# Two attention layers on one core: queries of two batches from one matmul of 288 columns

## The chip, the core and the metric

The kernel runs on one core of a Trainium2 chip. The core has a matmul engine (PE, with its weight loads listed as PEld), VectorE (DVE), ScalarE (ACT), GpSimd (POOL), and DMA queues; here SyncE (SP) issues nearly all transfers. The engines run side by side, each through its own list of instructions in order, and wait for one another by semaphores. The metric is the time of one execution in microseconds (us) on the device.

## The reference, cut to what matters

Two attention layers A and B of the same shapes, each with its own x, caches and weights, and their outputs beside each other:

```
x [16, 144, 448], wq [448, 16*256], k_cache and v_cache [16, 16, 512, 256], wo [16*256, 448]   (bf16)
q = (x @ wq) as [batch, head, 144, 256]
p = softmax(q @ k_cache^T / 16);  o = p @ v_cache
out[..., 0:448] of layer A, out[..., 448:896] of layer B = (heads of o side by side) @ wo
```

## The kernel before, in words

**Units and slots.** A unit U is one batch and one head of one layer: 512 units, 256 for each layer, in the order that `unit` (from L231) gives: batch by batch with its 16 heads, but for the first 32, where batches 0 and 1 are mixed. The program is written out by a loop over slots i, from -8 to 511 and a little beyond. In slot i unit i is finished, and the steps of later units are put beside it: this sets the order of each engine's list. One slot in the middle holds on PE, in this order:

- Q (`t_q`, L411): the query of unit i+15, transposed, x @ wq for 256 columns of Wq in two chunks of 128: eight matmuls of 144 columns (four pieces of the 448 rows of Wq by two chunks), into the PSUM bank qp_ps. `t_evac_q` (L425 on DVE, L429 on ACT) scales it by 1/16 into `qt_sb`, slot U % 12; DVE does it in slots i with i % 8 in 2, 4, 6, 7, ACT in the others.
- SB (`t_sb`, L459), in every eighth slot (i % 8 = 3): the scores of the last 32 query rows of eight units, four packed into one pass of the array.
- SA (`t_sa`, L536): the scores of the first 112 query rows of unit i+5, two matmuls of 512 columns, into one of the two banks sa_ps. Then DVE takes the maximum (`t_max`, L548) and ACT the exponential with its row sum (`t_exp`, L559).
- TA (`t_ta`, L590): four transposes of the probabilities of unit i+2 into sa_ps, which DVE copies to `pt_sb` (L600). Between exponential and TA lie the reciprocal (DVE, L569) and the division by the sum (POOL, L577). TB (`t_tb`, L513) does the same for the 32-row part, in two of eight slots.
- PV (`t_pv`, L623): the probabilities by V for unit i, eight matmuls of 144 columns; ACT copies the result into `ring` (L638, L640).
- OP (`t_op_piece`, L661): the output projection, matmuls of 448 columns for row chunks of 128 whose batches are finished. A credit of 2.25 matmuls per slot lets them out in twos (more from slot 482 on). The first chunk is ready in slot 25; where all ready chunks are done, a slot has no OP.

The 32-row part has its own maximum (L473), exponential (`t_exp_b`, L483, in the slots with i % 8 = 4 and 6, at the start of ACT's list for that slot) and reciprocal (L493).

**The plan of query slots.** `q_slot` gives the slot of each Q: eight in slot -7, one each in -5 to 2, two each in 4 to 7, then unit u in slot u-15. For units below 24 odd ones use the bank op_ps and even ones qp_ps (`q_bank`, L395), later ones qp_ps alone. A PSUM bank is guarded as a whole: a Q waits until the Q before it in the same bank is evacuated. In slots from 4 on the Qs stand at the start of the slot, one behind the other.

**Loads.** All loads are put in SP's list in the order of a deadline in slots (`plan`). K comes by DMA transposes for eight units at a time (L379), into one of three buffers, and occupies SP while it is issued; V (L392) for four units at a time, into one of three buffers, so a V load waits until PV of the units three groups earlier is done. x comes transposed for four batches at a time (L299, L300), into one of three buffers; the first four batches are loaded as they are and transposed on PE (`t_xt`, L336, copied out at L343): 12 transposes at the start, eight in slot 10. Wq lies once in the on-chip memory, in four parts of four heads (`t_load_wq`, L277 and L279); layer B's part goes in when the last Q of layer A that uses it is done, with deadlines 241, 245, 249 and 253, where its first Q stands. Wo (L287) likewise, in eight parts.

Of the kernel before, what the change touches and what calls it, by code (L numbers as in the profile page):

```python
# [5 lines left out]
BF16 = mybir.dt.bfloat16  # L6
# [116 lines left out]
def bass_concat_heads__mha_block_cached__gqa_block_cached__near_ridge_kernel(  # L123
# [54 lines left out]
    with contextlib.ExitStack() as es:  # L178
# [32 lines left out]
        x_nat = wo_flat[:, 8 * 4 * DH:8 * 4 * DH + 5 * D].rearrange("p (t e) -> p t e", t=5)  # L211
# [80 lines left out]

        def t_load_x(XG):
            pr, j = divmod(XG, Bn // XB)
            sl = XG % NXG
            x = xs[pr][j * XB:(j + 1) * XB].rearrange("b q d -> (b q) d")

            def e(q):
                q.dma_start_transpose(xt_sb[:, sl, 0:3, :], x[:, 0:384]).then_inc(sems["xt%d" % sl], 16)  # L299
                return q.dma_start_transpose(xt_sb[:, sl, 3, :], x[:, 320:448]).then_inc(sems["xt%d" % sl], 16)  # L300
            S.add(SP, e, writes=[(("xt", sl), XG)] + ([(("xt2", 0), 1)] if XG == NXG else []), dma_sem="xt%d" % sl, n_dma=2, name="x%d" % XG)

        def t_load_x_nat(k):
            x = xs[0][0:XB].rearrange("b q d -> (b q) d")
            sem = sems["xn%d" % k]

            def e(q):
                if k == 0:
                    return q.dma_start(x_nat[:, 0:3, :], x[0:384, :].rearrange("(t p) d -> p t d", p=128)).then_inc(
                        sem, 16)  # L310
                q.dma_start(x_nat[:, 3, :], x[384:512, :]).then_inc(sem, 16)
                return q.dma_start(x_nat[0:XB * SQ - 512, 4, :], x[512:XB * SQ, :]).then_inc(sem, 16)
            S.add(SP, e, writes=[(("xn", k), 0)], dma_sem="xn%d" % k, n_dma=1 + k, name="xn%d" % k)
# [10 lines left out]
        def t_xt(k):  # L324
            key, bank, acc = ((("sbb", 0), "sb0", ptb_ps[0]), (("sbb", 1), "sb1", ptb_ps[1]),
                              ("opp", "op", op_ps.bitcast(BF16)))[k]
            c0, n = ((0, 256), (256, 128), (384, XB * SQ - 384))[k]
            dst = acc[:, 0:4 * n].rearrange("p (c r) -> p c r", c=4)

            def e(t):  # L330
                ins = None
                for r0 in range(0, n, 128):
                    m = min(128, n - r0)
                    for kc in range(4):
                        d0 = min(128 * kc, D - 128)
                        ins = t.transpose(dst[:, kc, r0:r0 + m], x_nat[0:m, (c0 + r0) // 128, d0:d0 + 128],  # L336
                                          ident[0:m, 0:m])
                return ins
            S.add(PE, e, reads=[(("xn", k // 2), 0), ("ident", 0)], writes=[(key, ("x", k))], banks=[bank], name="XT%d" % k)

            def ev(v):
                o = xt_sb[:, 0, :, c0:c0 + n]
                return v.activation(o, dst, AF.Copy) if k == 1 else v.tensor_copy(o, dst)  # L343
            S.add(ACT if k == 1 else DVE, ev, reads=[(key, ("x", k))], writes=[(("xt2" if k == 2 else "xt", 0), 0)], banks=[bank],
                  name="ext%d" % k)
# [52 lines left out]
        def t_q(U):
            pr, b, h = unit(U)
            XG = (pr * Bn + b) // XB  # L400
            xsl = XG % NXG
            xo = (b % XB) * SQ
            hg = h // 4
            acc, key, bank = q_bank(U)

            def e(t):
                ins = None
                for kc in range(4):
                    for dc in range(2):
                        c0 = h * DH + dc * 128  # L410
                        ins = t.matmul(acc[:, dc * SQ:(dc + 1) * SQ], lhsT=wq_sb[:, kc, c0:c0 + 128],  # L411
                                       rhs=xt_sb[:, xsl, kc, xo:xo + SQ], start=(kc == 0 and dc == 0),
                                       stop=(kc == 3), skip_group_check=True)
                return ins
            S.add(PE, e, reads=[(("wq", hg), pr), ("wqz", 0), (("xt", xsl), XG)]
                  + ([(("xt2", 0), 0)] if XG == 0 and b > 1 else []),
                  writes=[(key, ("q", U))], banks=[bank], name="Q%d" % U)

        def t_evac_q(U):
            sl = U % NQT  # L420
            acc, key, bank = q_bank(U)
            src = acc[:, 0:2 * SQ].rearrange("p (c q) -> p c q", c=2)
            if (U - LQ) % 8 in (2, 4, 6, 7):
                def e(v):
                    return v.tensor_scalar(qt_sb[:, sl, :, :], src, 1.0 / 16.0, None, op0=ALU.mult)  # L425
                S.add(DVE, e, reads=[(key, ("q", U))], writes=[(("qt", sl), U)], banks=[bank], name="eq%d" % U)
            else:
                def e(a):
                    return a.activation(qt_sb[:, sl, :, :], src, AF.Copy, scale=1.0 / 16.0)  # L429
                S.add(ACT, e, reads=[(key, ("q", U))], writes=[(("qt", sl), U)], banks=[bank], name="eq%d" % U)  # L430
# [19 lines left out]
        def t_sb(SG):  # L450
            ksl = SG % NK

            def e(t):
                ins = None
                for dc in range(2):
                    for jj in range(8):
                        U = 8 * SG + jj
                        j = jj % 4
                        ins = t.matmul(sb_ps[jj // 4][32 * j:32 * j + 32, :].rearrange("q (k r) -> q k r", k=KR),  # L459
                                       lhsT=qt_sb[:, U % NQT, dc, QA:SQ],  # L460
                                       rhs=kt_of(U, dc), start=(dc == 0), stop=(dc == 1),
                                       tile_position=(0, 32 * j))
# [65 lines left out]
        def t_sa(U):  # L528
            SG = U // 8
            ksl = SG % NK  # L530
            bank = U % 2

            def e(t):
                ins = None
                for dc in range(2):
                    ins = t.matmul(sa_ps[bank][0:QA, :].rearrange("q (k r) -> q k r", k=KR),  # L536
                                   lhsT=qt_sb[:, U % NQT, dc, 0:QA],
                                   rhs=kt_of(U, dc), start=(dc == 0), stop=(dc == 1))
                return ins
            S.add(PE, e, reads=[(("qt", U % NQT), U)] + kt_keys([U]), writes=[(("sap", bank), ("s", U))],  # L540
# [166 lines left out]
        q_slot = [u - LQ for u in range(NT)]  # L707
        q_slot[0:24] = [-7] * 8 + [-5, -4, -3, -2, -1, 0, 1, 2] + [4, 4, 5, 5, 6, 6, 7, 7]
# [15 lines left out]
        for u in range(NT):  # L724
            at(q_at, q_slot[u], u)
# [3 lines left out]
        for XG in range(NXGT):  # L729
            pr, j = divmod(XG, Bn // XB)  # L730
            u_first = pr * NU + j * XB * H
            dl = u_first - LQ
            if XG >= NXG:
                pr0, j0 = divmod(XG - NXG, Bn // XB)
                lo = pr0 * NU + (j0 + 1) * XB * H - 1 - LQ + 1
            else:
                lo = s_min
            if XG:
                plan(lo, dl, 40, t_load_x, XG)
# [61 lines left out]
        while True:  # L801
# [10 lines left out]
            if i == q_slot[0]:  # L812
# [5 lines left out]
            for u in qs if not -LS <= i < 4 else ():  # L818
                t_q(u)
                t_evac_q(u)  # L820
                if i == q_slot[0] and u >= 3:
                    t_kt(u - 3)
# [44 lines left out]
            if i == 10:  # L867
                t_xt(2)
# [83 lines left out]
```

## Time and profile before

| | us |
|---|---|
| median of three runs | 1188.12 (1187.64 to 1190.12) |
| the profiled execution | 1193.1 |
| its span, first to last instruction | 1191.4 |
| granted clock of PE, mean | 1.000 |
| Q matmuls on qp_ps (L411), busy | 331.8 for 4000 |
| PV matmuls (L623), busy | 340.5 for 4096 |
| SA matmuls (L536), busy | 310.1 for 1024 |
| OP matmuls (L661) on op_ps, busy | 280.6 for 1120 |
| evacuations of Q on DVE (L425) | 112.8 for 247, mean 0.457 |
| evacuations of Q on ACT (L429) | 104.5 for 253, mean 0.413 |
| DMA, mean over the span | 247 GB/s |

How to read it: the profiled execution is one run with the profiler on; its time is a little over the runs', and the sums below are made against it. Busy times of PE overlap: a matmul's row covers its way through the array, while the next has begun. So what a matmul costs PE's queue is read from the distance between starts in the timeline. Behind a row of the timeline or of a group, square brackets give the time for which the engine stood idle before it and what ended that time. "SPq" is SP's list: the length of a row there is how long SP was held by issuing.

### The profile page before, as it was taken

Reading aid. Unit: us, or ns where it says so; the run is one execution under the profiler, and the core shown is the slowest. Engines: PE = TensorE matmul, PEld = TensorE weight load, DVE = VectorE, ACT = ScalarE, POOL = GpSimd, SP = SyncE. Lnnn points to the kernel's source line nnn. Section 1 sums busy time; section 2 is a strip of 40 time slices with the busy share of each in tenths; the row PEclk is TensorE's granted clock in tenths of the full one; section 3 lists DMA queues with packets and bytes.
Section 4 is the critical chain, followed back from the end, with each engine's and each line's share of the span. In section 5 each row is a group of like instructions: output and inputs, shape, how many; then the busy total and the mean of one; then the engine's idle time right before and its main releaser. Section 6 shows DMA issues by size and latency. Waiting matters only on the chain.

```text
span 1191.4 us, 34160 instructions
## 1 busy us (share of the span) xinstructions
PE 1178.3 (99%) x14116; PEld 902.6 (76%) x14116; DVE 776.0 (65%) x2192; ACT 754.9 (63%) x2220; POOL 676.3 (57%) x680
## 2 busy tenths in 40 slices
PE   8999999999999999999989999999999999999998
PEld 6777777777777777777767777777777777777775
DVE  5766667666666666666666666666766666666564
ACT  4766666666666666666656666666666666666564
POOL 2555556565565565565555655655655656656553
PEclk9999999999999999999999999999999999999999
DMA  9999999999989999999999999999999999998971
GB/s 343 235 298 279 272 270 234 243 243 253 255 219 246 229 264 249 221 235 244 273 281 286 270 279 277 249 238 233 248 254 234 231 243 250 248 236 238 238 190 48
DMA packets 611146, 294.09 MB, mean 247 GB/s; under 512 B 529712, under 2 KB 538736, under 8 KB 610992
## 3 DMA queue, kind: packets, MB, share of 16 engines
q1 hardware_dynamic: 609360, 288.01, 103.1%
q0 software_dynamic: 1632, 3.90, 1.0%
q8 instruction: 112, 1.84, 0.6%
q14 instruction: 42, 0.34, 0.1%
HBM read 153.61 MB, written 4.13 MB: 132 GB/s over the span
## 4 chain that ended last, share of the span: by engine, by line
PE 95%; DMA 2%; DVE 2%; ACT 0%; issue 0%; SPq 0%; POOL 0%; DVEq 0%; POOLq 0%
PE ot_ps L623 20%; PE qp_ps L411 20%; PE sa_ps L536 19%; PE op_ps L661 17%; PE sa_ps L590 8%; PE sb_ps L459 5%; PE sb_ps L513 2%; DMA kt_sb<-in_A_k_cache_dram 2%; DVE stat L548 1%; DMA wq_sb<-in_B_wq_dram 1%; PE sa_ps L440 0%; PE qp_ps L661 0%; PE op_ps L411 0%; DVE pt_sb L600 0%; DVE stat L473 0%; PE ot_ps L359 0%
## 5 line engine op out<-in xcount | busy, mean ns | idle before, releaser
L577 POOL TENSOR_TENSOR pa_sb<-pa_sb,stat 112x512 bf16<-112x512 bf16 x512 | 531.8, 1039 | 504.1 <-DVE stat L569 503.9
L559 ACT ACTIVATE pa_sb<-sa_ps,stat 112x512 bf16<-112x512 f32 x512 | 351.9, 687 | 404.7 <-DVE stat L548 403.4
L548 DVE TENSOR_REDUCE stat<-sa_ps 112x1 f32<-112x512 f32 x512 | 354.0, 691 | 328.4 <-PE sa_ps L536 327.7
L411 PEld LDWEIGHTS qp_ps<-xt_sb,wq_sb 128*128 128x128 bf16 x4000 | 281.9, 98 | 79.1 <-issue 3.5
L623 PE MATMUL ot_ps<-pt_sb,v_sb 128*128 128x144 bf16 x4096 | 340.5, 226 | 0.0
L411 PE MATMUL qp_ps<-xt_sb,wq_sb 128*128 128x144 bf16 x4000 | 331.8, 226 | 3.1 <-DMA wq_sb<-in_B_wq_dram 3.1
L536 PE MATMUL sa_ps<-kt_sb,qt_sb 128*112 128x512 bf16 x1024 | 310.1, 384 | 1.7 <-ACT pa_sb L559 0.7
L661 PE MATMUL op_ps<-wo_sb,ring 128*128 128x448 bf16 x1120 | 280.6, 352 | 0.0
L623 PEld LDWEIGHTS ot_ps<-pt_sb,v_sb 128*128 128x128 bf16 x4096 | 268.5, 97 | 0.4
L590 PEld LDWEIGHTS sa_ps<-ident,pa_sb 112*128 112x128 bf16 x2048 | 146.7, 97 | 108.2 <-ACT pa_sb L559 21.1
L638 ACT ACTIVATE ring<-ot_ps 128x288 bf16<-128x288 f32 (+8 forms) x512 | 189.9, 371 | 4.5 <-PE ot_ps L623 4.5
L600 DVE COPY pt_sb<-sa_ps 128x448 bf16<-128x448 bf16 x512 | 190.8, 373 | 2.4 <-PE sa_ps L590 2.4
L590 PE MATMUL sa_ps<-ident,pa_sb 112*128 112x112 bf16 x2048 | 185.4, 212 | 0.1
L425 DVE TENSOR_SCALAR qt_sb<-qp_ps 128x288 bf16<-128x288 f32 x247 | 112.8, 457 | 65.9 <-PE qp_ps L411 65.1
L501 POOL TENSOR_TENSOR pb_sb<-pb_sb,stat 128x512 bf16<-128x512 bf16 x128 | 132.9, 1038 | 0.7 <-DVE stat L493 0.7
L536 PEld LDWEIGHTS sa_ps<-kt_sb,qt_sb 128*112 128x112 bf16 x1024 | 97.2, 129 | 37.8 <-issue 27.2
L429 ACT ACTIVATE qt_sb<-qp_ps 128x288 bf16<-128x288 f32 x253 | 104.5, 413 | 15.9 <-PE qp_ps L411 14.8
L661 PEld LDWEIGHTS op_ps<-wo_sb,ring 128*128 128x128 bf16 x1120 | 94.7, 98 | 25.6 <-ACT ring L638 0.2
L559 ACT ACTIVATION_READ_ACCUMULATOR pa_sb<-sa_ps,stat 112x1 f32 x512 | 99.0, 193 | 0.0
L483 ACT ACTIVATE pb_sb<-sb_ps,stat 128x512 bf16<-128x512 f32 x128 | 88.4, 690 | 0.0
L473 DVE TENSOR_REDUCE stat<-sb_ps 128x1 f32<-128x512 f32 x128 | 87.2, 681 | 0.0
L569 DVE RECIPROCAL stat<-stat 112x1 f32<-112x1 f32 x512 | 78.4, 153 | 0.5 <-ACT pa_sb L559 0.5
(49 smaller groups left out, 426.3 us busy)
## 6 DMA issues: line engine op xcount, KB each, us to landing
v_sb<-in_A_v_cache_dram SPq DMA_DIRECT2D x64, 1024.0 KB, 6.0
v_sb<-in_B_v_cache_dram SPq DMA_DIRECT2D x64, 1024.0 KB, 6.0
out_dram<-ost_sb POOLq DMA_DIRECT2D x34, 112.0 KB, 6.1
wo_sb<-in_A_wo_dram SPq DMA_DIRECT2D x8, 448.0 KB, 8.1
wo_sb<-in_B_wo_dram SPq DMA_DIRECT2D x8, 448.0 KB, 6.9
wq_sb<-in_A_wq_dram SPq DMA_DIRECT2D x4, 768.0 KB, 11.0
wq_sb<-in_B_wq_dram SPq DMA_DIRECT2D x4, 768.0 KB, 7.6
kt_sb<-in_A_k_cache_dram SPq DMA_DIRECT2D x2, 1024.0 KB, 8.8
```

The lines of the kernel that those rows point to most:

```text
L411: ins = t.matmul(acc[:, dc * SQ:(dc + 1) * SQ], lhsT=wq_sb[:, kc, c0:c0 + 128], rhs=xt_sb[:, xsl, kc, xo:xo + SQ], start=(kc == 0 and dc = ...
L425: return v.tensor_scalar(qt_sb[:, sl, :, :], src, 1.0 / 16.0, None, op0=ALU.mult)
L501: return g.tensor_tensor(pb_sb[:, psl, :], pb_sb[:, psl, :], stat[:, RINVB + sl:RINVB + sl + 1].to_broadcast([128, SK]), op=ALU.mult)
L536: ins = t.matmul(sa_ps[bank][0:QA, :].rearrange("q (k r) -> q k r", k=KR), lhsT=qt_sb[:, U % NQT, dc, 0:QA], rhs=kt_of(U, dc), start=(dc = ...
L548: return v.tensor_reduce(stat[0:QA, NEG + sl:NEG + sl + 1], sa_ps[bank][0:QA, :], axis=AX.X, op=ALU.max, negate=True)
L559: return a.activation(pa_sb[0:QA, psl, :], sa_ps[bank][0:QA, :], AF.Exp, bias=stat[0:QA, NEG + sl:NEG + sl + 1], scale=1.0, accum_out=stat ...
L577: return g.tensor_tensor(pa_sb[0:QA, psl, :], pa_sb[0:QA, psl, :], stat[0:QA, RINV + sl:RINV + sl + 1].to_broadcast([QA, SK]), op=ALU.mult)
L590: ins = t.transpose(pta_ps[bank][:, c * 128:c * 128 + QA], src[:, c, :], ident[0:QA, 0:QA])
L600: return v.tensor_copy(pt_sb[:, sl, :, 0:QA], pta_ps[bank][:, 0:512].rearrange("p (c q) -> p c q", c=4)[:, :, 0:QA])
L623: ins = t.matmul(ot_ps[ob][:, dc * SQ:(dc + 1) * SQ], lhsT=v_sb[:, vsl, j, c * DH + dc * 128:c * DH + (dc + 1) * 128], rhs=pt_sb[:, sl, c, ...
L638: ins = a.activation(ring[:, 2 * h:2 * h + 2, c0:c0 + n1], src[:, :, 0:n1], AF.Copy)
L661: ins = t.matmul(acc[0:m, 0:D], lhsT=ring[:, c, col0:col0 + m], rhs=wo_sb[:, c, :], start=(c == first), stop=(c == last))
```

## The change

A group P is now two batches of one layer (16 groups). Item k of a group (32 items: head k // 2, chunk k % 2 of 128 columns) makes one chunk of the query of both batches with four matmuls of 288 columns, and one evacuation writes it to two query slots. So one item is as much arithmetic as one Q before, and there are 512 of either. With them come: 34 query slots in place of 12, given out from a list of free ones; x in groups of two batches in two buffers; the first four batches loaded as six tiles of 96 rows; banks qp_ps and op_ps in turn for group 0 alone; evacuation on DVE for k % 8 in 1, 3, 5, 6; and a new plan: group 0 in slots -7 to 10, group 1 (32 items) in slots 11 to 33, then group P from slot 32P-30 on, one item a slot, so that the last stands in slot 481. Wq of layer B has the deadlines 226, 234, 242 and 250.

```diff
-    NK, NV, NXG = 3, 3, 3
-    XB = 4 if Bn % 4 == 0 else (2 if Bn % 2 == 0 else 1)
-    NQT, NPA, NPB, NPT, NST, NSTB, NOST = 12, 5, 2, 8, 4, 2, 3
+    NK, NV, NXG = 3, 3, 2
+    XB = 2
+    NQT, NPA, NPB, NPT, NST, NSTB, NOST = 34, 5, 2, 8, 4, 2, 3
...
-        def q_bank(U):
-            return (op_ps, "opp", "op") if U < 24 and U % 2 else (qp_ps, "qp", "qp")
...
+        def t_q(P, k):
+            XG = P
+            pr, j = divmod(P, Bn // XB)
+            h, dc = divmod(k, 2)
+            us = [unit_of[(pr, XB * j + i, h)] for i in range(XB)]
+            if dc == 0:
+                qt_at[us[0]] = qt_free.pop(0)
+                qt_at[us[1]] = qt_free.pop()
+            lo, hi = qt_at[us[0]], qt_at[us[1]]
+            assert lo < hi
+            acc, key, bank = (op_ps, "opp", "op") if P == 0 and k % 2 else (qp_ps, "qp", "qp")
...
+                for kc in range(4):
+                    ins = t.matmul(acc[:, 0:XB * SQ], lhsT=wq_sb[:, kc, c0:c0 + 128], rhs=xt_sb[:, XG % NXG, kc, :],
+                                   start=(kc == 0), stop=(kc == 3))
...
+            src = acc[:, 0:XB * SQ].rearrange("p (b q) -> p b q", b=XB)
+            dst = qt_sb[:, lo:hi + 1:hi - lo, dc, :]
...
+            if k % 8 in (1, 3, 5, 6):
+                def ev(v):
+                    return v.tensor_scalar(dst, src, 1.0 / 16.0, None, op0=ALU.mult)
...
-        q_slot = [u - LQ for u in range(NT)]
-        q_slot[0:24] = [-7] * 8 + [-5, -4, -3, -2, -1, 0, 1, 2] + [4, 4, 5, 5, 6, 6, 7, 7]
+        q_slot = [[32 * P - 30 + k for k in range(32)] for P in range(NXGT)]
+        q_slot[0] = [-7] * 8 + [-5, -4, -3, -2, -1, 0, 1, 2] + [4, 4, 5, 5, 6, 6, 7, 7, 7, 8, 8, 8, 9, 9, 10, 10]
+        q_slot[1] = [11 + 23 * k // 32 for k in range(32)]
...
+        for XG in range(2, NXGT):
+            plan(q_slot[XG - NXG][31] + 1, 9.5 if XG == 2 else q_slot[XG][0] - 1, 40, t_load_x, XG)
         for pr in range(NP):
+            P0 = pr * Bn // XB
             for hg in range(HG):
-                dl = pr * NU + 4 * hg - LQ if pr > 0 else (-59, -56, -49, -48)[hg]
-                lo = pr * NU - H + 4 * hg + 3 - LQ + 1 if pr > 0 else s_min
+                dl = q_slot[P0][8 * hg] if pr > 0 else (-59, -56, -49, -48)[hg]
+                lo = q_slot[P0 - 1][8 * hg + 7] + 1 if pr > 0 else s_min
                 plan(lo, dl, 10 ** 6, t_load_wq, pr, hg)
...
-            if i == 10:
-                t_xt(2)
+            if i in (8, 9):
+                t_xt(i - 6)
```

More of the change, by code (lines that the diff above doesn't have):

```diff
@@ L210, in bass_concat_heads__mha_block_cached__gqa_block_cached__near_ridge_kernel @@
         kt1_nat = wo_flat[:, 0:8 * 4 * DH].rearrange("p (u c e) -> p u c e", u=8, c=4)
-        x_nat = wo_flat[:, 8 * 4 * DH:8 * 4 * DH + 5 * D].rearrange("p (t e) -> p t e", t=5)
+        x_nat = wo_flat[:, 8 * 4 * DH:8 * 4 * DH + 6 * D].rearrange("p (t e) -> p t e", t=6)
         kt_nat = (kt0_nat, kt1_nat)
@@ L300, in e @@
                 return q.dma_start_transpose(xt_sb[:, sl, 3, :], x[:, 320:448]).then_inc(sems["xt%d" % sl], 16)
-            S.add(SP, e, writes=[(("xt", sl), XG)] + ([(("xt2", 0), 1)] if XG == NXG else []), dma_sem="xt%d" % sl, n_dma=2, name="x%d" % XG)
+            S.add(SP, e, writes=[(("xt", sl), XG)], dma_sem="xt%d" % sl, n_dma=2, name="x%d" % XG)
         def t_load_x_nat(k):
-            x = xs[0][0:XB].rearrange("b q d -> (b q) d")
-            sem = sems["xn%d" % k]
+            x = xs[0][XB * k:XB * k + XB].rearrange("b q d -> (b q) d")
             def e(q):
[L308 to L313, printed above, removed]
+                return q.dma_start(x_nat[0:96, 3 * k:3 * k + 3, :], x.rearrange("(t p) d -> p t d", p=96)).then_inc(
+                    sems["xn%d" % k], 16)
+            S.add(SP, e, writes=[(("xn", k), 0)], dma_sem="xn%d" % k, name="xn%d" % k)
         def t_load_k_nat(hf):
@@ L324, in t_xt @@
         def t_xt(k):
-            key, bank, acc = ((("sbb", 0), "sb0", ptb_ps[0]), (("sbb", 1), "sb1", ptb_ps[1]),
-                              ("opp", "op", op_ps.bitcast(BF16)))[k]
-            c0, n = ((0, 256), (256, 128), (384, XB * SQ - 384))[k]
+            key, bank, acc = ("opp", "op", op_ps.bitcast(BF16)) if k > 1 else (("sbb", k), "sb%d" % k, ptb_ps[k])
+            t0, nt = ((0, 2), (2, 1))[k % 2]
+            n = nt * 96
             dst = acc[:, 0:4 * n].rearrange("p (c r) -> p c r", c=4)
@@ L331, in e @@
                 ins = None
-                for r0 in range(0, n, 128):
-                    m = min(128, n - r0)
+                for j in range(nt):
                     for kc in range(4):
                         d0 = min(128 * kc, D - 128)
-                        ins = t.transpose(dst[:, kc, r0:r0 + m], x_nat[0:m, (c0 + r0) // 128, d0:d0 + 128],
-                                          ident[0:m, 0:m])
-                return ins
-            S.add(PE, e, reads=[(("xn", k // 2), 0), ("ident", 0)], writes=[(key, ("x", k))], banks=[bank], name="XT%d" % k)
+                        ins = t.transpose(dst[:, kc, 96 * j:96 * j + 96],
+                                          x_nat[0:96, 3 * (k // 2) + t0 + j, d0:d0 + 128], ident[0:96, 0:96])
+                return ins
+            S.add(PE, e, reads=[(("xn", k // 2), 0), ("ident", 0)], writes=[(key, ("x", k))], banks=[bank],
+                  name="XT%d" % k)
             def ev(v):
-                o = xt_sb[:, 0, :, c0:c0 + n]
+                o = xt_sb[:, k // 2, :, 96 * t0:96 * t0 + n]
                 return v.activation(o, dst, AF.Copy) if k == 1 else v.tensor_copy(o, dst)
-            S.add(ACT if k == 1 else DVE, ev, reads=[(key, ("x", k))], writes=[(("xt2" if k == 2 else "xt", 0), 0)], banks=[bank],
+            S.add(ACT if k == 1 else DVE, ev, reads=[(key, ("x", k))], writes=[(("xt", k // 2), k // 2)], banks=[bank],
                   name="ext%d" % k)
@@ L393, in t_load_v @@
             S.add(SP, e, writes=[(("v", sl), G)], dma_sem="v%d" % sl, name="v%d" % G)
-        def q_bank(U):
-            return (op_ps, "opp", "op") if U < 24 and U % 2 else (qp_ps, "qp", "qp")
[L398 to L404, printed above, removed]
+        unit_of = {unit(U): U for U in range(NT)}
+        qt_free = list(range(NQT))
@@ L406, in e @@
+        qt_at = {}
+        def t_q(P, k):
[9 more added lines that the diff above has]
+            acc, key, bank = (op_ps, "opp", "op") if P == 0 and k % 2 else (qp_ps, "qp", "qp")
             def e(t):
@@ L407, in e @@
                 ins = None
+                c0 = h * DH + dc * 128
                 for kc in range(4):
[L409 to L413, printed above, removed]
-                return ins
@@ L415, in t_q @@
[L415 to L426, printed above, removed]
-            else:
-                def e(a):
-                    return a.activation(qt_sb[:, sl, :, :], src, AF.Copy, scale=1.0 / 16.0)
-                S.add(ACT, e, reads=[(key, ("q", U))], writes=[(("qt", sl), U)], banks=[bank], name="eq%d" % U)
+                    ins = t.matmul(acc[:, 0:XB * SQ], lhsT=wq_sb[:, kc, c0:c0 + 128], rhs=xt_sb[:, XG % NXG, kc, :],
+                                   start=(kc == 0), stop=(kc == 3))
@@ new lines, in e, with ev @@
+                return ins
+            S.add(PE, e, reads=[(("wq", h // 4), pr), ("wqz", 0), (("xt", XG % NXG), XG)],
+                  writes=[(key, ("q", P, k))], banks=[bank], name="Q%d" % (32 * P + k))
+            src = acc[:, 0:XB * SQ].rearrange("p (b q) -> p b q", b=XB)
+            dst = qt_sb[:, lo:hi + 1:hi - lo, dc, :]
+            w = [(("qt", lo), us[0]), (("qt", hi), us[1])]
+            if k % 8 in (1, 3, 5, 6):
+                def ev(v):
+                    return v.tensor_scalar(dst, src, 1.0 / 16.0, None, op0=ALU.mult)
+                S.add(DVE, ev, reads=[(key, ("q", P, k))], writes=w, banks=[bank], name="eq%d" % (32 * P + k))
+            else:
+                def ev(a):
+                    return a.activation(dst, src, AF.Copy, scale=1.0 / 16.0)
+                S.add(ACT, ev, reads=[(key, ("q", P, k))], writes=w, banks=[bank], name="eq%d" % (32 * P + k))
@@ L432, in kt_of, with qt_done, qt_key @@
+        qt_used = {}
+        def qt_done(U):
+            qt_used[U] = qt_used.get(U, 0) + 1
+            if qt_used[U] == 2:
+                qt_free.append(qt_at[U])
+                qt_free.sort()
+        def qt_key(U):
+            return (("qt", qt_at[U]), U)
         def kt_of(U, dc):
@@ L450, in t_sb @@
         def t_sb(SG):
-            ksl = SG % NK
+            qe = [qt_at[8 * SG + jj] for jj in range(8)]
+            for jj in range(8):
+                qt_done(8 * SG + jj)
             def e(t):
@@ L459, in e @@
                         ins = t.matmul(sb_ps[jj // 4][32 * j:32 * j + 32, :].rearrange("q (k r) -> q k r", k=KR),
-                                       lhsT=qt_sb[:, U % NQT, dc, QA:SQ],
+                                       lhsT=qt_sb[:, qe[jj], dc, QA:SQ],
                                        rhs=kt_of(U, dc), start=(dc == 0), stop=(dc == 1),
@@ L463, in e @@
                 return ins
-            S.add(PE, e, reads=[(("qt", (8 * SG + jj) % NQT), 8 * SG + jj) for jj in range(8)]
+            S.add(PE, e, reads=[qt_key(8 * SG + jj) for jj in range(8)]
                   + kt_keys(range(8 * SG, 8 * SG + 8)),
@@ L529, in t_sa @@
             SG = U // 8
-            ksl = SG % NK
             bank = U % 2
+            qe = qt_at[U]
+            qt_done(U)
             def e(t):
@@ L536, in e @@
                     ins = t.matmul(sa_ps[bank][0:QA, :].rearrange("q (k r) -> q k r", k=KR),
-                                   lhsT=qt_sb[:, U % NQT, dc, 0:QA],
+                                   lhsT=qt_sb[:, qe, dc, 0:QA],
                                    rhs=kt_of(U, dc), start=(dc == 0), stop=(dc == 1))
                 return ins
-            S.add(PE, e, reads=[(("qt", U % NQT), U)] + kt_keys([U]), writes=[(("sap", bank), ("s", U))],
+            S.add(PE, e, reads=[qt_key(U)] + kt_keys([U]), writes=[(("sap", bank), ("s", U))],
                   banks=["sa%d" % bank], name="SA%d" % U)
@@ L723, in bass_concat_heads__mha_block_cached__gqa_block_cached__near_ridge_kernel @@
                 at(tb_at, max(s0 + 3, 8 * n - 4 + 4 * h), G)
-        for u in range(NT):
-            at(q_at, q_slot[u], u)
+        for P in range(NXGT):
+            for k in range(32):
+                at(q_at, q_slot[P][k], (P, k))
         for u in range(NKT):
@@ L728, in bass_concat_heads__mha_block_cached__gqa_block_cached__near_ridge_kernel @@
         s_min = -8
[L729 to L739, printed above, removed]
+        for XG in range(2, NXGT):
+            plan(q_slot[XG - NXG][31] + 1, 9.5 if XG == 2 else q_slot[XG][0] - 1, 40, t_load_x, XG)
         for pr in range(NP):
+            P0 = pr * Bn // XB
             for hg in range(HG):
-                dl = pr * NU + 4 * hg - LQ if pr > 0 else (-59, -56, -49, -48)[hg]
-                lo = pr * NU - H + 4 * hg + 3 - LQ + 1 if pr > 0 else s_min
+                dl = q_slot[P0][8 * hg] if pr > 0 else (-59, -56, -49, -48)[hg]
+                lo = q_slot[P0 - 1][8 * hg + 7] + 1 if pr > 0 else s_min
                 plan(lo, dl, 10 ** 6, t_load_wq, pr, hg)
@@ L811, in bass_concat_heads__mha_block_cached__gqa_block_cached__near_ridge_kernel @@
                 t_store(stores.pop(0)[0])
-            if i == q_slot[0]:
+            if i == q_slot[0][0]:
                 t_warm(0)
@@ L817, in bass_concat_heads__mha_block_cached__gqa_block_cached__near_ridge_kernel @@
             qs = q_at.get(i, ())
[L818 to L822, printed above, removed]
+            for P, k in qs if not -LS <= i < 4 else ():
+                t_q(P, k)
+                if i == q_slot[0][0] and k >= 3:
+                    t_kt(k - 3)
             for n in sbs.get(i, ()):
@@ L829, in bass_concat_heads__mha_block_cached__gqa_block_cached__near_ridge_kernel @@
                 t_exp(u)
-            for u in qs if -LS <= i < 4 else ():
-                t_q(u)
-                t_evac_q(u)
+            for P, k in qs if -LS <= i < 4 else ():
+                t_q(P, k)
             u = i + LS - 1
```

## The prediction

> **What bounds the kernel now.** I read the page first, then the order of instructions on each engine.
>
> ```profile
> PE 1178.3 (99%) x14116; PEld 902.6 (76%) x14116; DVE 776.0 (65%) x2192; ACT 754.9 (63%) x2220; POOL 676.3 (57%) x680
> PE 95%; DMA 2%; DVE 2%; ACT 0%; issue 0%; SPq 0%; POOL 0%; DVEq 0%; POOLq 0%
> ```
>
> PE is busy 99% of the span and 95% of the chain that ended last: what lengthens or shortens PE's queue moves the end. The timeline of PE shows one whole slot (start, length, operation):
>
> ```profile
> 682.78 0.66 PE L411 MATMUL qp_ps<-xt_sb,wq_sb 128*128 128x144 bf16 x8
> 683.28 0.59 PE L536 MATMUL sa_ps<-kt_sb,qt_sb 128*112 128x512 bf16 x2
> 683.71 0.36 PE L590 MATMUL sa_ps<-ident,pa_sb 112*128 112x112 bf16 x4
> 683.91 0.67 PE L623 MATMUL ot_ps<-pt_sb,v_sb 128*128 128x144 bf16 x8
> 684.41 0.54 PE L661 MATMUL op_ps<-wo_sb,ring 128*128 128x448 bf16 x2
> 684.79 0.66 PE L411 MATMUL qp_ps<-xt_sb,wq_sb 128*128 128x144 bf16 x8
> ```
>
> Starts, not lengths, give the price: Q takes 0.50 (8 x 62.5 ns), SA 0.43 (2 x 215), TA 0.20, PV 0.50, two matmuls of the output projection (OP) 0.38; 2.01 us with no gap. Where a slot has no OP (7 to 24, 487 to 495 and a few between), another chain binds: SA, maximum and copy on DVE, then SA of the next slot. The slots at 45.75 and 1152.86 have neither Q nor OP and last 1.56 and 1.55 us, 0.43 over the matmuls' 1.13, and the second shows who was late:
>
> ```profile
> 1152.86 0.66 PE L623 MATMUL ot_ps<-pt_sb,v_sb 128*128 128x144 bf16 x8
> 1153.74 0.64 PE L536 MATMUL sa_ps<-kt_sb,qt_sb 128*112 128x512 bf16 x2 [0.22 <-DVE pt_sb L600]
> 1154.41 0.67 PE L623 MATMUL ot_ps<-pt_sb,v_sb 128*128 128x144 bf16 x8
> ```
>
> From SA to SA that chain takes 1.73 to 1.78 us (44.90 to 46.63, 46.63 to 48.41, 1151.96 to 1153.74). So Q work taken out of a slot without OP saves little, and Q work added to one is partly covered.
>
> **1. Wider matmuls: -5.4 us.** Spacing is 62.5 ns at 144 columns, 190 at 448, 215 at 512; the line through them gives 122 to 123 at 288. A Q of four costs 0.49 us instead of 0.50, 10.5 ns x 512 = 5.4. Evacuations stay 512 of 288 columns (457 ns on DVE, 413 on ACT); two pieces in place of one is a form not shown for this tile, but the evacuation into the ring writes two pieces and takes 401, so I take 0 (bounds -0.01 and +0.05 us each, off PE's path). The Trainium skill (TensorE: Matmul & The Clock Gate, section Back-to-back issue gap) gives a sustained spacing of about 81 ns at 128 columns and 131 at 512; by it (my interpolation, an estimate) a Q falls from 8 x 83 to 4 x 102 ns, 131 us in all. The trace disagrees already, with 62.5 and 215.
>
> **2. Query work moves forward: 15 Qs.** At slot i from 33 on, i+31 are made instead of i+16: six more in slots 7 to 10, nine more in 11 to 33, none after 481 instead of 496. At 0.50 us that is **+7.5** ahead of slot 35, given back as far as the tail lets it (5).
>
> **3. One bank for two Qs in a slot: +8.6.** From group 1 on every Q uses qp_ps. In slots 11, 13, 16, 18, 21, 23, 26, 28 and 31 two stand back to back on PE; the second waits until the first is evacuated, and SA, TA and PV queue behind it. Before, such pairs alternated qp_ps and op_ps. What an evacuation takes, without OP on ACT and with OP on DVE:
>
> ```profile
> 62.14 0.66 PE L411 MATMUL qp_ps<-xt_sb,wq_sb 128*128 128x144 bf16 x8
> ```
> ```profile
> 63.05 0.40 ACT L638 ACTIVATE ring<-ot_ps 128x288 bf16<-128x288 f32 x1
> 63.34 0.41 ACT L429 ACTIVATE qt_sb<-qp_ps 128x288 bf16<-128x288 f32 x1
> ```
>
> Here it ends 1.61 us after the Q began (it queues behind ex and the copy of PV's result); with 0.05 to restart PE (DVE copy at 46.58, SA at 46.63) less the Q's own 0.49, PE stands 1.17. On DVE (Q at 684.79, evacuation to 685.95) 0.72; on ACT with OP (682.78, 683.89) 0.67. By the change's k%8 the first of the pair goes to ACT in slots 11, 16, 18 (3 x 1.2 = 3.6), 31 (0.7) and 28, where ACT's exponential of the B rows stands ahead (by the rows of term 4 it would end at 692.2 for a Q begun at 690.30: 1.9 + 0.05 - 0.49 = 1.5), and to DVE in 13, 21, 23, 26 (2.9): 8.7. In 13 and 23 the first Q itself waits too for an ACT evacuation behind such an exponential (0.6 + 0.25). Six of the nine lie in slots without OP, whose present wait of about 0.15 goes: -0.9. In slots 7 to 10 the third Q of a slot waits for the first (about 0.6 and 0.35), and one each in 9 and 10 for the copy of transposed x out of op_ps (0.35 and 0.45), while 0.6 of idle time there is filled: **+1.2**. Bounds of the nine pairs together: all at 0.67 less cover, 5.1; all at 1.5, 13.
>
> By then PE is 17.3 us later, so a wait of before disappears, **-1.8**:
>
> ```profile
> 106.04 1.05 PE L459 MATMUL sb_ps<-kt_sb,qt_sb 128*32 128x512 bf16 x16 [1.73 <-DMA kt_sb<-in_A_k_cache_dram]
> ```
>
> That K load follows V loads which wait for PV of slots 15 and 23, and a new x load of at most 5 us is put ahead of it; I put its landing at 115 to 118 us instead of 106, PE's need at 122. Sum up to slot 35: 7.5 + 8.6 + 1.2 - 1.8 = +15.5.
>
> **4. Evacuations change engine: +4.** DVE had slots 2, 4, 6, 7 (mod 8), now 3, 5, 7, 0; ACT gets 4 and 6, where it also has the exponential of the B rows.
>
> ```profile
> 691.12 0.69 ACT L483 ACTIVATE pb_sb<-sb_ps,stat 128x512 bf16<-128x512 f32 x1
> 691.69 0.20 ACT L483 ACTIVATION_READ_ACCUMULATOR pb_sb<-sb_ps,stat 128x1 f32 x1
> 692.16 0.69 ACT L559 ACTIVATE pa_sb<-sa_ps,stat 112x512 bf16<-112x512 f32 x1 [0.26 <-DVE stat L548]
> ```
>
> Behind it an evacuation would end at 692.2, and PE's next Q begins at 692.31: in time, with OP, by 0.05 us. Without OP it isn't: such an exponential ends at 56.71 and the next Q began at 56.52, so that Q would come 0.55 late. Between slots 35 and 481 the timeline has 6 such slots of the first kind (0.55 to 0.8 each) and 9 of the second (0.35 to 0.55): 8.2 gross. About half is taken out of waits of SA that these slots have already. Bounds 0 and 8.2; I take 4.
>
> **5. The tail gives back -3.7.** Slots 482 to 486 have 4 to 10 matmuls of OP and give the full 5 x 0.50. The nine from 487 to 495 last 17.6 us; by the chain of 1.75 they last 8 x 1.75 + 2.4 for the one with SB = 16.4 without Q: 1.2.
>
> **6. Wq of layer B: -3.1 + 0.7.** In the DMA queue's timeline the fourth load stands behind a K transpose of 17 us, and PE waited for it:
>
> ```profile
> 573.81 17.18 SPq L379 DMA_TRANSPOSE kt_sb<-in_B_k_cache_dram  x1
> 591.03 0.58 SPq L392 DMA_DIRECT2D v_sb<-in_A_v_cache_dram  x1
> 591.66 0.50 SPq L277 DMA_DIRECT2D wq_sb<-in_B_wq_dram  x1
> ```
> ```profile
> 601.71 0.66 PE L411 MATMUL qp_ps<-xt_sb,wq_sb 128*128 128x144 bf16 x8 [3.10 <-DMA wq_sb<-in_B_wq_dram]
> ```
>
> That 3.1 goes. Each load now stands right behind a K transpose, ten slots ahead of its Q. For the first: V at 514.1, half an x transpose (5.1 / 2 = 2.6), K 11, two issues 1.1, 6.5 to 7 to land: 535.5 to 536.5, needed at 536.2. The others have no x load ahead and 1 to 3 us to spare. I take 0.7; bounds 0 and 4 x 0.75.
>
> The x loads for two batches halve a transpose and double their number: the same bytes in a queue that waits for V's buffers anyway (6 to 7 us per period of V issue time). x_nat in six tiles of 96 rows has 24 transposes instead of 20, under 0.2 us. A query slot is reused only after SA of an earlier slot, which PE has passed: no wait.
>
> **Sum.** -5.4 + 15.5 + 4 - 3.7 - 3.1 + 0.7 = **+8.0 us**. The profiled execution took 1193.1 us (span 1191.4 and 1.7 around it) and becomes 1201.1; the runs' median is 5.0 lower, 1188.1, and becomes **1196**.
>
> **Rivals.** What a measurement of this kernel can tell from no change is about 0.2%, 2.4 us: 1185.7 to 1190.5.
> (a) The pairs are covered (faster): slots 11 to 34 are set by the DVE chain and the DMA queue, not by PE. Then terms 3 and 4 are near 0 and the sum is 8.0 - 8.6 - 1.2 - 4 = -5.8: 1182; it decides when PE's stall per pair is under about 0.2 us. For it: six pairs lie in slots without OP. Against it: those slots have only 0.15 us of wait to give, and an evacuation alone is 0.41. Chance 0.11.
> (b) All small terms at their low ends (pairs 5.1, no term 4): 8.0 - 3.5 - 4 - 0.7 = about 0, 1188, within 0.2%. Chance 0.12.
> (c) The spread Wq loads come late all four times, 2 to 3 us each, since every one has a K transpose ahead, which took 11 to 17 us: 1204. For it: the 17.18 row came with a full queue. Against it: 11 to 12 is usual. Chance 0.10.
> (d) Matmuls are spaced by weight loads, so that half as many halve Q's cost: a load lasts 98 ns, and 8 x 98 against 4 x 122 would save 0.29 x 512 = 150 us, 1046. The spacing of 62.5 ns speaks against it. The section Back-to-back issue gap of the Trainium skill's TensorE: Matmul & The Clock Gate would have it so in part. Chance 0.01.
> The forecast, 1192 to 1202, has 0.66. Faster 0.12 (a, d), same 0.12 (b), slower 0.76. The range leaves out (a), (d) and the end of (c): 1187.5 to 1203.5.
>
> **What would show it.** Q at 0.49 in the slot's starts; nine gaps of 0.7 to 1.5 us before L411-type matmuls between 52 and 115 us, put down to the evacuation on ACT or DVE; slot 35 about 15 us later; no wait for K there; no 3.1 at Wq of B; slots 487 to 495 about 1.2 us shorter. Wrong if these gaps are missing, or if the last slots give back 7 us.

## The result and the profile after

The changed kernel takes 1204.1 us (median; 1203.99 to 1204.51), the kernel before 1188.08 beside it: ratio 1.0132, interval 1.0115 to 1.015. It is slower, as forecast, but by 16.0 us instead of 8, and lies 0.6 us above the top of the range of 1187.5 to 1203.5. The profiled execution took 1204.5 us (span 1202.8), so here it agrees with the other runs; for the kernel before it lay 5.0 us above them (1193.1 against 1188.1). So a profiled execution does not by itself take longer than a run, as the reading given with the profile before has it. That matters below.

The page after, the two rows that answer to those of before:

```profile
PE 1177.5 (98%) x12072; PEld 847.9 (70%) x12072; DVE 787.0 (65%) x2193; ACT 743.3 (62%) x2220; POOL 676.6 (56%) x680
PE 90%; DVE 5%; ACT 4%; issue 1%; POOL 0%; DVEq 0%; POOLq 0%
```

PE has 2044 matmuls fewer and is busy as long as before, but it carries only 90% of the chain that ended last: 9% now belong to DVE and ACT, and the 2% of DMA are gone. A slot in the middle, in the timeline of PE (start, length, operation), has no gap:

```profile
751.09 0.65 PE L411 MATMUL qp_ps<-xt_sb,wq_sb 128*128 128x288 bf16 x4
751.58 0.59 PE L547 MATMUL sa_ps<-kt_sb,qt_sb 128*112 128x512 bf16 x2
752.01 0.36 PE L601 MATMUL sa_ps<-ident,pa_sb 112*128 112x112 bf16 x4
```

Q takes 0.49 us. Where the time came from is read by setting the start of PV in each slot against the same slot before:

| slot | before | after | later by |
|---|---|---|---|
| 6 | 43.40 | 43.58 | 0.2 |
| 11 | 54.24 | 59.88 | 5.6 |
| 34 | 102.38 | 119.13 | 16.75 |
| 35 | 107.69 | 122.63 | 14.9 |
| 248 | 588.03 | 605.14 | 17.1 |
| 256 | 608.54 | 622.60 | 14.1 |
| 480 | 1115.95 | 1130.74 | 14.8 |
| 496 | 1152.86 | 1164.28 | 11.4 |
| end of span | 1191.4 | 1202.8 | 11.4 |

So on the profiled executions the change costs 11.4 us; 4.6 more come between the profiled executions and the runs.

**The pairs.** Slot 16 in the timeline of PE:

```profile
69.25 0.65 PE L411 MATMUL qp_ps<-xt_sb,wq_sb 128*128 128x288 bf16 x4
70.91 0.66 PE L411 MATMUL qp_ps<-xt_sb,wq_sb 128*128 128x288 bf16 x4 [1.01 <-ACT qt_sb L425]
71.41 0.59 PE L547 MATMUL sa_ps<-kt_sb,qt_sb 128*112 128x512 bf16 x2
```

The second Q begins 1.66 us after the first, 1.17 later than it could, and waits for the evacuation on ACT. (The 1.01 in brackets counts from the end of the first Q's last matmul on its way through the array.)

**The engines of the evacuations.** Slot 93 follows a slot that has the exponential of the B rows on ACT and no output projection. First PE (PV of slot 92, then Q of slot 93), then ACT:

```profile
251.26 0.67 PE L634 MATMUL ot_ps<-pt_sb,v_sb 128*128 128x144 bf16 x8
252.53 0.66 PE L411 MATMUL qp_ps<-xt_sb,wq_sb 128*128 128x288 bf16 x4 [0.60 <-ACT qt_sb L425]
```
```profile
251.38 0.70 ACT L493 ACTIVATE pb_sb<-sb_ps,stat 128x512 bf16<-128x512 f32 x1
251.95 0.22 ACT L493 ACTIVATION_READ_ACCUMULATOR pb_sb<-sb_ps,stat 128x1 f32 x1
252.04 0.43 ACT L425 ACTIVATE qt_sb<-qp_ps 128x288 bf16<-128x288 f32 x1
```

PV began at 251.26 and its eight matmuls take 0.50; the next Q could start at 251.76 and starts at 252.53, when ACT has done the exponential, its sum and only then the evacuation.

**Slot 35 and Wq.** The wait for K at slot 35 is gone (Q at 120.39, SB at 120.97), and so is that for Wq: the waits view of this profile lists no wait of PE for a transfer. The loads stand behind K transposes as planned:

```profile
549.84 13.66 SPq L375 DMA_TRANSPOSE kt_sb<-in_A_k_cache_dram  x1
563.54 0.58 SPq L277 DMA_DIRECT2D wq_sb<-in_B_wq_dram  x1
564.17 0.49 SPq L279 DMA_DIRECT2D wq_sb<-in_B_wq_dram  x1
```

**The tail.** Slots 487 to 495 are set by the DVE chain, each SA waiting for the copy of the slot before; from SA to SA 1.78 us:

```profile
1156.26 0.64 PE L547 MATMUL sa_ps<-kt_sb,qt_sb 128*112 128x512 bf16 x2 [0.44 <-DVE pt_sb L611]
1158.04 0.64 PE L547 MATMUL sa_ps<-kt_sb,qt_sb 128*112 128x512 bf16 x2 [0.44 <-DVE pt_sb L611]
```

### The profile page after: what moved, and what is told of

Its sections match the earlier page's. It is cut to its first block, busy times and chain, and to the rows that moved or that the text cites. A ratio compares the mean times of both kernels' runs of the same rounds, so it can differ in the third digit from the quotient of the medians.

```text
span 1202.8 us, 30088 instructions
## 1 busy us (share of the span) xinstructions
PE 1177.5 (98%) x12072; PEld 847.9 (70%) x12072; DVE 787.0 (65%) x2193; ACT 743.3 (62%) x2220; POOL 676.6 (56%) x680
## 4 chain that ended last, share of the span: by engine, by line
PE 90%; DVE 5%; ACT 4%; issue 1%; POOL 0%; DVEq 0%; POOLq 0%
PE qp_ps L411 19%; PE ot_ps L634 19%; PE sa_ps L547 18%; PE op_ps L672 17%; PE sa_ps L601 7%; PE sb_ps L469 5%; DVE stat L559 3%; PE sb_ps L523 2%; ACT pa_sb L570 2%; ACT pb_sb L493 1%; DVE qt_sb L421 1%; ACT qt_sb L425 1%; ACT ring L649 1%; PE sa_ps L447 1%; PE qp_ps L672 0%
## 5 line engine op out<-in xcount | busy, mean ns | idle before, releaser
L411 PE MATMUL qp_ps<-xt_sb,wq_sb 128*128 128x288 bf16 x1984 | 324.6, 286 | 13.7 <-ACT qt_sb L425 11.0
L411 PEld LDWEIGHTS qp_ps<-xt_sb,wq_sb 128*128 128x128 bf16 x1984 | 187.3, 98 | 122.0 <-ACT qt_sb L425 25.9
L601 PEld LDWEIGHTS sa_ps<-ident,pa_sb 112*128 112x128 bf16 x2048 | 148.3, 97 | 106.9 <-ACT pa_sb L570 14.8
L547 PEld LDWEIGHTS sa_ps<-kt_sb,qt_sb 128*112 128x112 bf16 x1024 | 120.9, 129 | 53.9 <-DVE qt_sb L421 24.2
L425 ACT ACTIVATE qt_sb<-qp_ps 128x288 bf16<-128x288 f32 x252 | 104.4, 414 | 15.7 <-PE qp_ps L411 14.9
```

Source lines behind the costliest of these rows:

```text
L411: ins = t.matmul(acc[:, 0:XB * SQ], lhsT=wq_sb[:, kc, c0:c0 + 128], rhs=xt_sb[:, XG % NXG, kc, :], start=(kc == 0), stop=(kc == 3))
L601: ins = t.transpose(pta_ps[bank][:, c * 128:c * 128 + QA], src[:, c, :], ident[0:QA, 0:QA])
```

## Experiments

Ratios are to the kernel before, which ran beside each experiment on the same chip. The kernel before had medians of 1188.1 (with the changed kernel), 1190.7 (e1 to e4), 1189.4 (e5 to e8) and 1189.5 (e9, e10). The changed kernel's 1204.1 was measured beside the first alone, so where an experiment is set against it, the profiles of the two are compared as well.

**e1, e2, e6: where the 5.0 us between the profiled execution of before and its runs lies.** e1 changes nothing.

> The kernel before, unchanged, profiled once more. The sum of the prediction was carried from the profiled execution (1193.1 us) to the runs (median 1188.1) with one constant of 5.0 us; the changed kernel shows no such constant (profiled 1204.5, runs 1204.1). Theory W: the 5.0 is the two waits for transfers that the profile of before shows (1.8 for K at slot 35, 3.1 for Wq of layer B), and undisturbed executions do not have them. Then this profile shows either both waits and a time near 1193, or neither and a time near 1188. Rival V: every execution has the waits, and the 5.0 lies elsewhere; then the waits show at any total, 1188 too.

Measured: 1192.4 us, span 1190.7. Neither both waits nor none: the wait for K at slot 35 is not there (slots 34 to 35 take 3.5 us instead of 5.3, 0.6 of it coming back in the next slot), that for Wq is, in its waits view:

```profile
PE qp_ps L411 <- DMA wq_sb<-in_B_wq_dram: 2.6, 1, 2.6
PE ot_ps L623 <- DMA v_sb<-in_A_v_cache_dram: 0.5, 1, 0.5
```

So the waits come one by one and differ between executions of one program. The nine runs beside it spread from 1188.2 to 1192.1.

Here the wait for Wq has a second cost. Behind it the profile shows a granted clock of PE of 0.50 from 599.6 to 603.0 us, and 1.00 before and after. The matmuls stand almost twice as far apart, Q at 0.92 us and SA at 0.85 instead of 0.50 and 0.43:

```profile
599.62 1.12 PE L411 MATMUL qp_ps<-xt_sb,wq_sb 128*128 128x144 bf16 x8 [2.61 <-DMA wq_sb<-in_B_wq_dram]
600.54 1.06 PE L536 MATMUL sa_ps<-kt_sb,qt_sb 128*112 128x512 bf16 x2
601.39 0.58 PE L590 MATMUL sa_ps<-ident,pa_sb 112*128 112x112 bf16 x4
```

Against e6 below, which has no such wait, slots 253 and 254 lose 4.2 us for a wait of 2.6. In the first profile the wait was longer, 3.1 us, the clock stayed at 1.00, and only 3.3 were lost. What decides whether the clock falls is not shown.

e2 moves Wq's loads ahead:

```diff
-                dl = pr * NU + 4 * hg - LQ if pr > 0 else (-59, -56, -49, -48)[hg]
+                dl = pr * NU + 4 * hg - LQ - 8 if pr > 0 else (-59, -56, -49, -48)[hg]
```

> The kernel before with the deadlines of layer B's four Wq loads 8 slots earlier (233 + 4 for each), so that the fourth stands ahead of the K transpose of 17 us and not behind it. Theory W: the wait of 3.1 us for Wq goes from the profile, but the runs stay at 1188 (ratio 0.999 to 1.001), since they had no such wait. Rival V: the runs fall by about 3 us, ratio 0.9975.

Measured: 1198.6 us, ratio 1.0069 (1.0055 to 1.0082): slower, which neither theory had. The wait for Wq is gone, but the first Wq load, which has to wait until its part is free, now stands ahead of a K transpose, and this begins at 543.0 us instead of 532.5; a transpose of x behind it held SP for 8.0 us (3.7 in the first profile). SB of slot 243 waits for the next K:

```profile
PE sb_ps L459 <- DMA kt_sb<-in_A_k_cache_dram: 7.8, 2, 7.6
```

Here too the granted clock is 0.50, from 577.8 to 588.1 us, and slots 243 and 244 lose 10.2 us against e6 for the wait of 7.6. All five runs have a mean clock of 0.996 or 0.997. The experiment says nothing between W and V, and shows that the order of loads at the change of layers had no room for such a move in the kernel before.

e6 gives the last quarter of layer B's Wq a buffer of its own:

```diff
+        wqs_sb = sb("wqs_sb", [128, 4, 4 * DH], BF16)
...
+                if pr > 0 and hg == HG - 1:
+                    lo, dl = 180, 200
                 plan(lo, dl, 10 ** 6, t_load_wq, pr, hg)
```

> The kernel before, with a buffer of its own for the last quarter of layer B's Wq, loaded 40 slots ahead (and x in two buffers instead of three to make room; one more memset on POOL at the start). Neither this quarter nor the K transpose behind it is then pressed for time. Theory W (the waits for transfers in the kernel before differ from run to run, 0 to 5 us, and its fastest runs have none): Wq's wait is gone from the profile, the runs lie at 1187.5 to 1189 and closer together, whatever the kernel before does on the same chip. Rival V (every run has the 3.1): 1184.5 to 1185.

Measured: 1188.2 us (11 runs, 1187.7 to 1191.2), ratio 0.9994 (0.9985 to 1.0003). Its profiled execution is one of these runs, 1188.2 with a span of 1186.5, and has neither wait: against the first profile PV is 1.8 us earlier at slot 35 and 3.3 more at slot 256. Rival V wanted 1184.5 to 1185, and falls. Take the two waits from the first profile and its 1193.1 become 1188.0, the runs' median. "Closer together" holds for eight of the eleven, 1187.7 to 1188.8; three are at 1189.8 to 1191.2, and what these three waited for was not traced (the longest has a mean clock of 0.998, as e1 has; the other ten have 1.0).

**e3: the evacuation engines.**

```diff
-            if k % 8 in (1, 3, 5, 6):
+            if k % 8 in ((1, 3, 5, 6) if P < 2 else (0, 2, 4, 5)):
```

> The changed kernel, but from group 2 on the evacuations go to DVE for k % 8 in 0, 2, 4, 5, which are the slots 2, 4, 6, 7 (mod 8) of before; ACT no longer has one in the slots with its exponential of the B rows. Theory A: the jumps of 0.26 to 0.57 us at the slots 5 and 7 (mod 8) without output projection, 6.9 us in the profile between slots 35 and 481, all go: about 1197.3, ratio to before 1.008. Rival B: they come from writing the queries in two pieces, or from reading them from more places, and stay: 1204, ratio 1.013. Rival C: half of them move to SA waiting for DVE: about 1201.

Measured: 1197.15 us (1196.98 to 1197.33), ratio 1.0059 (1.0046 to 1.0072). That is 6.95 us under the changed kernel, and the profile says where: at 20 slots, the very ones at which the changed kernel lost time, it is earlier by 0.06 to 0.55, together 6.95, and by 0.2 in all the others together. Slot 93 again, timeline of PE of e3:

```profile
250.32 0.67 PE L634 MATMUL ot_ps<-pt_sb,v_sb 128*128 128x144 bf16 x8
250.82 0.65 PE L411 MATMUL qp_ps<-xt_sb,wq_sb 128*128 128x288 bf16 x4
251.42 0.64 PE L547 MATMUL sa_ps<-kt_sb,qt_sb 128*112 128x512 bf16 x2
```

Q follows PV after 0.50. Theory A holds, B and C fall: writing the queries in two pieces costs the path nothing (and the evacuations last 456 and 414 ns, against 457 and 413 in the kernel before).

**e4: two banks for the pairs of slots 11 to 23.**

```diff
+            second = P == 1 and k > 0 and q_slot[1][k - 1] == q_slot[1][k] < 25
-            acc, key, bank = (op_ps, "opp", "op") if P == 0 and k % 2 else (qp_ps, "qp", "qp")
+            acc, key, bank = (op_ps, "opp", "op") if P == 0 and k % 2 or second else (qp_ps, "qp", "qp")
```

> The changed kernel, but in the six pairs of slots 11, 13, 16, 18, 21 and 23 the second query goes to the bank op_ps, which is idle until slot 25. Theory A: PE's standstills of 0.7 to 1.2 us between the two of a pair go, 5.8 us in all, of which SA's wait for the DVE chain takes back 0.9: about 1199, ratio 1.009. Rival D (slots 11 to 24 are set by the chain over DVE, not by PE): the standstill only moves behind the pair, at most 1 us is won, 1203.

Measured: 1198.1 us (1198.05 to 1198.85), ratio 1.0069 (1.0056 to 1.0081): 6.0 less. In the profile each pair gives back its standstill in full, 1.18 in slots 11, 16 and 18 and 0.72 or 0.73 in 13, 21 and 23, 5.7 in all. Slot 16, timeline of PE of e4:

```profile
66.97 0.65 PE L412 MATMUL qp_ps<-xt_sb,wq_sb 128*128 128x288 bf16 x4
67.46 0.65 PE L412 MATMUL op_ps<-xt_sb,wq_sb 128*128 128x288 bf16 x4
67.95 0.59 PE L548 MATMUL sa_ps<-kt_sb,qt_sb 128*112 128x512 bf16 x2
```

The two Qs stand 0.49 apart. Rival D, by which DVE would hold the pairs back, falls.

**e5: the width alone.**

```diff
-                    ins = t.matmul(acc[:, 0:XB * SQ], lhsT=wq_sb[:, kc, c0:c0 + 128], rhs=xt_sb[:, XG % NXG, kc, :],
-                                   start=(kc == 0), stop=(kc == 3))
+                    for bb in range(XB):
+                        ins = t.matmul(acc[:, bb * SQ:(bb + 1) * SQ], lhsT=wq_sb[:, kc, c0:c0 + 128],
+                                       rhs=xt_sb[:, XG % NXG, kc, bb * SQ:(bb + 1) * SQ],
+                                       start=(kc == 0 and bb == 0), stop=(kc == 3), skip_group_check=True)
```

> The changed kernel with its whole plan, but each item by eight matmuls of 144 columns (two batches by four pieces) in place of four of 288. Theory A (matmuls cost their columns and 2.5 ns each): 10.5 ns more for each of 512 items, 4.6 to 5.4 us: about 1209, ratio to the changed kernel 1.004. Rival E (the weight load sets the spacing): far more, over 100 us. Rival F (the width is hidden anyway): 1204.

Measured: 1208.8 us (1208.05 to 1208.9), ratio 1.0159 (1.0143 to 1.0174): 4.7 more than with wide matmuls, 9.1 ns an item. The profile shows it as an even drift, 4.1 us over 445 slots, with no step. E and F fall. So the one gain that the wider matmuls bring is 4.7 us, and the plan that they need costs more.

**e7, e8: both losses mended, and the tail.** e7 is e3 and e4 together, with the pairs of group 1 moved out of the slots that have output projection:

```diff
-        q_slot[1] = [11 + 23 * k // 32 for k in range(32)]
+        q_slot[1] = [11 + 14 * k // 23 for k in range(23)] + list(range(25, 34))
```

> The changed kernel with the evacuation engines of e3, and the nine pairs of group 1 all in slots 11 to 23, with the second of a pair in op_ps (slots 25 to 33 have one item each). Theory A: 7.0 from the engines and 8 from the pairs (nine pairs that cost about 0.35 us each instead of 12.2 in all): 1188.5 to 1190, as fast as the kernel before. Rival D (the DVE chain holds the pairs back): 1193.

Measured: 1187.6 us (11 runs, 1187.1 to 1188.0), ratio 0.998 (0.9971 to 0.9989), but against runs of before with their transfer waits; against the 1188.2 of e6 it is level. In the profile, against e6, slots 11 to 24 now rise by 0.33 to 0.48 us for eight of the nine pairs, and not at all for the first, in slot 11.

e8 adds:

```diff
-            if i >= u_tail0 - 14:
+            if i >= u_tail0:
                 credit += 4.0
```

> e7 with the faster output projection starting at slot 496 instead of 482, so that slots 482 to 495, which have no query work any more, get about two of its matmuls each. Theory G (in a slot without Q the DVE chain of 1.75 us sets the time, and 0.38 us of output projection is free): the fifteen slots 481 to 495, 31.6 us in the changed kernel, shrink to about 28.5: 1185.5 to 1187, a little under the kernel before. Rival H: the projection that is put off comes back behind slot 496, and nothing is won: 1188.5 to 1190.

Measured: 1185.3 us (1185.0 to 1185.7), ratio 0.9964 (0.9951 to 0.9977): 2.3 under e7. H falls: behind slot 496 the profile is 0.3 shorter and not longer. Theory G holds for the place, not for the whole size: in the profile the fifteen slots 481 to 495 shrink from 31.5 us to 29.75, not to 28.5. Slots without Q in the timeline of PE of e8, from SA to SA 1.78 us with two matmuls of projection as well as without:

```profile
1127.26 0.64 PE L548 MATMUL sa_ps<-kt_sb,qt_sb 128*112 128x512 bf16 x2
1127.73 0.36 PE L602 MATMUL sa_ps<-ident,pa_sb 112*128 112x112 bf16 x4
1127.93 0.67 PE L635 MATMUL ot_ps<-pt_sb,v_sb 128*128 128x144 bf16 x8
1128.43 0.54 PE L673 MATMUL op_ps<-wo_sb,ring 128*128 128x448 bf16 x2
1129.04 0.64 PE L548 MATMUL sa_ps<-kt_sb,qt_sb 128*112 128x512 bf16 x2
```

**e9: the same later start in the kernel before** (the same two lines).

> The kernel before with the same later start of the faster output projection (slot 496 instead of 482). Theory G: here the slots 487 to 495 still hold a Q of 0.50, so a slot with two matmuls of projection is PE's 2.01 against the 1.78 it takes without; only the 0.15 or so of SA's wait in each of nine slots can be filled: 1.3 us, ratio 0.999. Rival I (the gain of e8 has nothing to do with the missing queries): 2.3 us as in e8, ratio 0.998.

Measured: 1188.6 us (12 runs, 1186.6 to 1191.4), ratio 0.9993 (0.9984 to 1.0002): 0.9 by the medians, an interval that includes 1, so the runs leave G's 1.3 open and speak against I's 2.3. In the profile the stretch from slot 482 to the end is 1.25 us shorter than before; in e8 it is 2.1 shorter than in e7.

**e10: two query items in a slot.** e8 with the last sixteen items of group 0 spread evenly:

```diff
-[4, 4, 5, 5, 6, 6, 7, 7, 7, 8, 8, 8, 9, 9, 10, 10]
+[3, 3, 4, 4, 5, 5, 6, 6, 7, 7, 8, 8, 9, 9, 10, 10]
```

> e8 with the last sixteen items of group 0 in slots 3 to 10, two in each, instead of 2, 2, 2, 3, 3, 2, 2 in slots 4 to 10, so that none is the third of its slot and waits for the first. Theory A: of the rise of 4.5 us between slots 6 and 11 about 0.9 goes, 1184.4. Rival J: slot 3 waits for the third part of Wq (which landed at 33 us, slot 3 has its Qs at 36) or is slowed by the K transposes on PE there: 1185.3 or more.

Measured: 1184.4 us (1184.1 to 1185.0), ratio 0.9961 (0.9949 to 0.9974), 0.9 under e8. From slot 6 to 8 its PV gains 1.8 us on e8's, having lost 0.9 in slot 3 to the two Qs there. Theory A's number comes out and J falls. It is the fastest kernel here, 3.8 us under e6, the kernel before without its wait for Wq. Not all of that belongs to the wider matmuls: the later projection, which the kernel before can have as well, gave 1.25 us in the profile of e9.

## Why the prediction was wrong

The direction and nearly every mechanism were right; the size was half of what came. By the steps, on the profiled executions:

| step | forecast | trace |
|---|---|---|
| 1, wider matmuls | -5.4 | -4.4 (e5: 4.5 in its profile, 4.7 in runs) |
| 2 and 3, work ahead, pairs, slots 7 to 10 | +17.3 | +17.2 |
| 3, wait for K at slot 35 | -1.8 | -1.8 |
| 4, evacuation engines | +4 | +6.9 |
| 5, tail | -3.7 | -3.4 |
| 6, Wq, old wait and new | -3.1 + 0.7 | -3.3 + 0 |
| start | 0 | +0.2 |
| sum | +8.0 | +11.4 |

(The 17.2 is the 16.75 of slot 34, less 0.2 of the start, with 0.6 that wider matmuls had saved by then; that 0.6 is an estimate from the 3.8 us that they save between slots 35 and 480.)

Of the 8.0 us by which the result exceeds the forecast, 3.4 lie in this sum, 2.9 of them in step 4, and 4.6 in the way from the profiled executions to the runs.

**The step that failed first is the last one of the sum**, "the runs' median is 5.0 lower, 1188.1, and becomes 1196". The 5.0 us was taken for a constant between a profiled execution and a run. In that one execution it was two waits for transfers, 1.8 for K and 3.3 around Wq: e6 shows a profiled execution without them at its runs' median, e1 one with only the second, and the changed kernel, which has none, shows no distance. That the runs at 1188.1 had neither is argued from this and not traced. For them, then, the -1.8 of step 3 and the -3.1 of step 6 were no gains. Without them the same working gives 8.0 + 4.9 = 12.9, and the trace's 11.4 becomes 16.5, where 16.0 was measured. The sign in the page was there: runs from 1187.64 to 1190.12 and a profiled execution at 1193.1, with two waits that sum to the difference.

The 1188.1 is itself a base at the low end, and with it the 16.0 owes something to luck. The three traced executions with this order of loads (the first, e1 and e9) all waited for Wq, 2.6 to 3.1 us, and of the 46 runs of the kernel before beside the experiments 11 took at most 1188.8, which 8 of the 11 of e6 do. So most runs seem to have a part of the waits. Against the later medians of 1189.4 to 1190.7 the change would cost 13.4 to 14.7 us, and not 16.0.

**The second is the term of step 4**, "about half is taken out of waits of SA that these slots have already". The places and their gross size were about right: 15 slots and 8.2 us forecast gross, and in the trace eight slots that lose 0.54 to 0.57, seven that lose 0.26 to 0.32 and five smaller ones, net. So 6.9 stayed, about five sixths of the 8.2. A late Q is covered only as far as its slot had a wait to give: in slot 93 Q comes 0.77 us late, the slot took 1.83 before where its matmuls need 1.63, and it gets 0.57 longer. e3 takes the whole 6.95 back.

Step 5, that query work in the tail is nearly free and comes back only in part, is right to 0.3 us; step 2 was measured only in its sum with step 3. Step 3's price of a pair (1.17 behind ACT, 0.72 behind DVE) is what e4 gave back, 1.18 and 0.72. What did not happen: rival (a), by which the pairs are covered (e4 against it); (b), small terms at their low ends; (c), since no Wq load came late; (d), since e5 moves 4.7 us and not 150. What stays open is the half microsecond between 16.5 and 16.0, and what the three longer runs of e6 waited for.

## What to carry to other kernels

Before a sum is carried from a profiled execution to runs, look for waits on transfers in that execution that a run need not have: a gain that removes such a wait may be no gain. Where runs of one program spread by some us, compare with more than a few of them. Where two groups of matmuls for the same PSUM bank stand back to back in PE's list, and the bank is guarded as a whole, the second waits for a whole evacuation with the queue ahead of it on its engine. Here that was 0.72 to 1.18 us a pair, paid in full even in slots that another chain seemed to set (e4). A fusion that halves the instructions but needs the work earlier has to be paid for at both ends: look first at what fills the slots it empties (e8) and how the slots it fills are arranged (e4, e10).

## What the runs showed of the hardware that was not expected

Transfers are far less even than the engines. The same K transpose at the change of layers held SP for 17.2, 17.9 and 17.0 us in three executions (the first profile, e1 and e6), and the one ahead of it, of the same size, for 11.0, 9.2 and 9.2. A transpose of x of one size took 3.7 and 6.4 us at two places of the first profile, and 8.0 in e2. Where PE waits for nothing, its own times repeat to about 0.01 us a slot from profile to profile, so that two profiles can be laid beside each other slot by slot and each step of a few hundredths read off.

A wait of PE can cost more than its length. With a wait of 2.6 us in e1 the granted clock fell to 0.50 for 3.4 us, and 4.2 us were lost. With one of 7.6 us in e2 it fell for 10.2 us, beginning while PE still stood, and the two slots lost 10.2 us. With a wait of 3.1 us in the first profile it stayed at 1.00.
